# A fused linear-attention and mixture kernel: the written-out order of all engines is replaced by another one

## The chip, the cores and the metric

The kernel runs on one core of a Trainium2 chip. The metric is the device time of one launch in microseconds (us); lower is better. Each of the core's engines works through a queue of its own, and semaphores tie the queues together: TensorE (PE) multiplies matrices, VectorE (DVE), ScalarE (ACT) and GpSimd (POOL) work elementwise, SyncE (SP) issues the transfers.

## The reference

Two stages. A recurrence with a state of 48x48 for each of 4x8 heads runs over 768 steps; its output, 384 wide, goes through four attention experts, of which the two with the largest gate count for a row.

```python
for t in range(S):                                   # S = 768, D = 48
    cur = einsum('bhd,bhe->bhde', u * k[t], v[t])
    y[t] = einsum('bhd,bhde->bhe', r[t], state + cur)
    state = w[t][..., None] * state + einsum('bhd,bhe->bhde', k[t], v[t])
x = y as (B, S, 384)
logits = x @ w_gate                                  # E = 4 experts, the top 2 kept
for e in range(E):                                   # Hd = 64
    q, k, v = x @ wq[e], x @ wk[e], x @ wv[e]
    a = softmax(causal(q @ k.T / 8))
    ye = a @ v @ wo[e]
    out += gate weight of e (if in the top 2) * ye
```

## The kernel before

The work is cut into eight units, a batch and a half of the sequence (384 steps) each. In a unit the recurrence goes over four pairs of heads. The 384 steps of a pair are taken in six chunks of 64: DVE and POOL build products of decays (`w`, `suf`), decayed keys (`kt`) and decayed receptances (`pre`) from the loaded tile `lt`; PE transposes the keys (`ktp`, copied to `kts`), forms what each chunk adds to the state (`ups`), and the products of scores inside a chunk (`aps`, masked into `am`, one `aps` for two pairs of heads); DVE carries the state over the six chunks, one update `wst = wst * suf + ups` each (L366), so that each update reads the one before it of the same pair; PE joins state and scores to the output (`yps`). The bonus term with `u` is a reduction over a head, `rk`, on DVE (L499, one instruction) or on ACT (L497, six), and a scaling of the values with it, `ux` (L506, six instructions on ACT). Then a unit's `xn` is transposed (`xp`, copied to `xh` and `xl`) and goes through the experts: projections of queries and keys (`pp`, L625), values and gate logits (`vp`, L657, copied to `v_sb`), scores (`sp`, L721), maximum on DVE and exponential on ACT (`a`), transposes of `a` (`tp`, copied to `ATa` and `ATb`), the product with the values (`yp`, L778), gates, and the output projection (`op`, L846).

What runs on which engine, and in which order, isn't decided by a scheduler. `Plan.add` numbers some 2,100 operations and notes what each reads and writes. A table, `ORDER`, lists them all as a letter for the engine and a number (`V` DVE, `A` ACT, `P` PE, `G` POOL, `S` SP, `X` left out), and `Plan.order` walks that table; the engines' queues are this list taken apart. Buffers are handed out along the list, the one that has been free longest first:

```python
        for e, n in listed:
            o = ops[n]
            for s in o["slots"]:
                if s.idx is None and e:
                    s.idx = free[s.tag].pop(0)
            o["e"] = o["how"] = e
            if e == "PE":
                o["how"] = last = way(last, o["mode"])
            finish(o)
```

PE's operations have a mode: `F` uses the whole array, `Q`, `S`, `T` and `V` use tilings of it (`Q` 64x64, `S` and `T` 64 rows, `V` 64 columns). A transpose runs in 64-row pieces or, where the operation ahead of it uses the whole array (`way`), in one piece. A load on SP waits for the last PE operation but one that stands ahead of it in the list. Ten multiplications at the start (`warm`) have no reader.

Of the kernel before, what the change touches and what calls it, by code (L numbers as in the profile page):

```python
# [941 lines left out]
S110 S111 V2 V1 V117 V118 V119 V114 S3 V121 V120 V123 P5 S136 S197 S112 V139 V142 V122 V143 V146 V144 V148 V147 V145 V149 S137 S113 P6 S170 V176 V173  # L942
V177 V180 V178 V124 V182 S171 P7 S195 P8 P115 P9 P126 P140 A127 A141 A116 A0 P128 P10 S138 S235 P151 A152 P11 P12 P153 P13 A125 A129 P14 P185 A186
P187 A150 S99 A188 V130 S250 V154 V155 V156 V157 V158 V159 V131 V132 V133 V134 P161 G181 G198 G206 G205 V160 V243 V238 V179 G135 V164 V162 V189 G201
V183 X165 X163 P174 A175 P199 A200 V190 S289 V202 V207 S196 V239 V203 V204 V258 V208 V253 V254 P166 A167 P210 V211 V191 V240 S172 S4 P168 A169 P229
A209 A230 A184 G242 V244 V192 V241 V257 P212 G259 G194 S236 S251 P220 V193 V213 V214 V215 V216 V217 V297 G292 G219 G296 S304 V218 V221 P265 X222 P225
V223 V255 V293 S290 V246 V247 V256 V245 V261 V260 V262 X224 P227 A267 S367 A266 P268 A226 S352 A100 P231 A232 A228 A248 P1131 P1066 P233 P1127 P1067
P1070 P1128 P1071 A263 A234 A249 A102 A264 V269 V275 V270 V276 V271 V272 V294 V277 G298 G307 V273 V312 V300 V278 V308 S305 V311 V313 V295 G274 G299
G374 V279 V309 P281 V284 V282 S104 S252 P1068 P1129 S237 P319 P1072 P1132 P1133 X285 X283 V310 V370 V280 V355 V314 V301 V371 A320 A1069 A1130 A1073
A321 P335 A338 A1134 A105 P322 S368 V315 V356 V316 P1086 P1087 P1088 V329 V323 V317 V324 V330 V331 V325 V302 A1089 A318 G101 G359 S306 G360 G361 P286  # L950
V336 S291 V326 V327 V332 A303 S353 V287 V333 V288 X337 V378 G334 G328 G339 S408 S423 G376 P1074 P1097 P1106 P1115 V1098 V1100 V1109 V1091 V1107 V357
V1118 P343 A1101 A1090 P1075 P1104 A344 A1119 V1116 V345 P1080 P1081 P1076 P1082 A1108 A1099 A1117 P1122 A1084 A1105 A1123 V358 V103 V106 P340 P1111
A1077 A1110 A1083 A1078 A1112 G363 V341 V1085 V342 V372 V1079 V375 V411 V1092 V379 V373 V362 V416 P1120 A1121 P1113 P1102 S369 A1114 A1103 P382 P349
P346 S409 A383 P1124 P1125 P1126 A350 A347 A384 P385 A386 A393 A1165 A380 V351 V348 G377 P1135 P1144 V430 V412 V426 V415 G364 G1093 G419 S473 G431
P1259 P1260 P1261 V1136 V1147 V387 V1138 V394 V413 S107 V388 V395 V1145 V389 A1137 A1148 A381 A1262 A1094 A1139 P400 V401 V403 P1195 P1196 P1197 P1151
V414 V417 S488 V427 P1153 A1152 P1142 A1198 X404 X402 G418 G432 V396 V428 V397 S424 S354 V1156 V390 V398 V1154 V391 V429 V420 V433 P1205 P1191 P1192
P1193 P1206 P1207 A365 A1143 A1146 P1149 S410 V480 V1095 A1194 S542 A1157 A1150 A1209 P1222 P1140 A366 A1141 A1208 A1155 V421 P456 P1211 P1212 P1213
V1225 V1223 V457 G399 G1096 G476 X458 P1231 A459 P1160 S527 A108 A1161 V434 V477 V491 V392 V1232 V1234 V478 G460 G495 P1158 P438 P405 V435 V482 V479
V1167 V1210 V492 A422 A440 A439 A1159 P441 V407 V1216 S489 V406 V442 V449 V450 V443 V451 V444 V493 V452 V436 A1226 A1235 P1162 P1163 P1164 A1215 A1166
A1214 A1224 P1242 G549 G1168 G497 G481 G109 G483 P1169 P1263 P1264 A1233 A437 V445 V1170 V1243 V446 V453 V447 V454 P1171 P1265 S425 P1239 V1172 S474  # L960
V1245 V494 V496 V499 V498 V545 G455 P503 A1266 A1240 A1173 A504 A1241 A505 P1175 P1199 P1200 P1201 P1229 A1230 A1203 P1236 A1237 A1238 V1176 V530
A1177 G448 G1178 G534 G550 G1174 G535 G500 G484 S605 P519 P1227 P1267 A1228 A1202 A1244 A1246 V520 V522 P506 P461 X523 X521 V1204 V1268 V513 V1270
V507 V508 V463 V509 V510 V514 S490 V511 V515 V516 V462 V517 V531 V485 S543 S590 V532 V546 V1217 V533 V536 S592 P1247 P1179 P1180 P1183 P1184 P1250
A1248 A1249 A501 A1185 A1251 A1252 A502 P1276 P467 S528 A468 V1279 V1277 V469 V486 V547 A1280 A1181 P1253 P1254 P1255 G551 G593 G1218 G518 P470 P557
P464 A471 A465 V472 V466 V537 V553 V548 V512 S475 V538 V608 A559 A1219 A558 V554 P1256 P1257 P1258 P1284 A1304 S661 A1269 A1271 A1285 A1286 P1287
# [138 lines left out]
```

## Time and profile before

| | |
|---|---|
| median of 3 runs | 325.13 us (324.5 to 327.95) |
| the profiled execution | 323.68 us |
| its span, first to last instruction | 321.9 us |
| PE busy | 308.9 us |
| DVE busy | 265.3 us |
| ACT busy | 237.2 us |
| POOL busy | 133.6 us |

The median is what counts. The profiled execution is one more run, and durations and waits below are its own. "Busy" is the time in which at least one instruction of an engine ran; PE's instructions overlap in its pipeline, so the distance from one start to the next says what one costs.

### The profile page before, as it was taken

The numbers are of one execution on the slowest core, as the hardware profiler recorded it, in microseconds if no ns is written. First come the engines' busy times: TensorE is split into PE (matmuls) and PEld (weight loads), VectorE is DVE, ScalarE is ACT, GpSimd is POOL, SyncE is SP. The second block draws the span as 40 slices with busy tenths as digits, with TensorE's granted clock in tenths as the row PEclk, the third lists the DMA queues.
The fourth block names the chain that finished last, engine by engine and source line by source line (L and its number), as shares of the span: only waits on it lengthen the run. The fifth ranks groups of instructions, "written<-read, shape, count | busy, mean of one in ns | idle before, by whom it ended". The sixth has DMA issues, their size and how long they took to land.

```text
span 321.9 us, 12978 instructions
## 1 busy us (share of the span) xinstructions
PE 308.9 (96%) x5179; PEld 245.1 (76%) x5179; DVE 265.3 (82%) x872; ACT 237.2 (74%) x835; POOL 133.6 (42%) x267
## 2 busy tenths in 40 slices
PE   4989999998999999999999999998999999999995
PEld 2678677876877987898768767997769686777775
DVE  6998999999999999999988899986774745637743
ACT  1526988899989988887889888455978546775762
POOL 2224454545655446635555755285622010120220
PEclk9987999999999999999999999999999999999999
DMA  7687655674554564665571474340200010001022
GB/s 249 238 289 250 213 184 207 200 245 131 150 171 149 176 222 155 214 219 136 163 256 36 158 275 119 119 131 22 95 2 2 24 52 2 0 4 49 2 100 73
DMA packets 18204, 44.13 MB, mean 137 GB/s; under 512 B 2144, under 2 KB 10080, under 8 KB 18144
## 3 DMA queue, kind: packets, MB, share of 16 engines
q1 hardware_dynamic: 18144, 43.30, 41.6%
q8 instruction: 41, 0.67, 0.9%
q14 instruction: 19, 0.16, 0.2%
HBM read 38.58 MB, written 4.72 MB: 135 GB/s over the span
## 4 chain that ended last, share of the span: by engine, by line
PE 80%; DVE 13%; DMA 2%; issue 2%; ACT 1%; SPq 0%
PE pp L625 14%; PE yp L778 12%; PE sp L721 12%; PE op L846 8%; PE vp L657 7%; PE tp L184 5%; PE tp L180 4%; PE aps L532 4%; PE ups L355 3%; PE yps L310 3%; PE yps L308 3%; DVE wst L366 2%; DMA lt<-in_wkr_dram 2%; DVE am L537 2%; DVE suf L467 2%
## 5 line engine op out<-in xcount | busy, mean ns | idle before, releaser
L736 ACT ACTIVATE a<-a,mx 128x128 f32<-128x128 f32 (+5 forms) x96 | 64.2, 671 | 8.4 <-DVE mx L731 8.1
L731 DVE CUSTOM_DVE_ANT_0 a<-sp,causal 128x128 f32<-128x128 f32 (+5 forms) x96 | 56.9, 618 | 14.8 <-PE sp L721 9.0
L188 ACT COPY ATa<-tp 128x512 f32<-128x512 f32 (+3 forms) x79 | 36.9, 482 | 16.7 <-PE tp L184 11.0
L721 PE MATMUL sp<-K,Q 64*128 64x384 f32 (+4 forms) x256 | 46.3, 471 | 0.0
L366 DVE SCALAR_TENSOR_TENSOR wst<-wst,suf,ups 112x48 f32<-112x48 f32 x160 | 37.2, 257 | 2.1 <-PE ups L355 0.4
L506 ACT ACTIVATE xn<-nat,rk 128x48 f32<-128x48 f32 x156 | 37.8, 330 | 0.4 <-DVE rk L499 0.4
L778 PE MATMUL yp<-ATa,v_sb 128*64 128x384 f32 (+2 forms) x240 | 35.6, 430 | 0.0
L625 PE MATMUL pp<-xh,wh_qk 128*128 128x384 f32 x84 | 31.1, 371 | 0.0
L625 PE MATMUL pp<-xh,wl_qk 128*128 128x384 f32 x84 | 28.3, 337 | 0.0
L625 PE MATMUL pp<-xl,wh_qk 128*128 128x384 f32 x84 | 28.3, 337 | 0.0
L184 PEld LDWEIGHTS tp<-ident,a 64*128 64x128 f32 x456 | 19.6, 138 | 11.0 <-ACT ATa L188 3.2
L721 PEld LDWEIGHTS sp<-K,Q 64*128 64x128 f32 x256 | 20.8, 187 | 8.8 <-issue 2.3
L310 PE MATMUL yps<-ys,pre 64*64 64x48 f32 (+1 forms) x704 | 25.1, 222 | 1.2 <-issue 1.2
L308 PE MATMUL yps<-vy,am 64*64 64x48 f32 x768 | 25.5, 222 | 0.0
L778 PEld LDWEIGHTS yp<-ATa,v_sb 128*64 128x64 f32 x240 | 15.2, 136 | 12.7 <-issue 9.9
L310 PEld LDWEIGHTS yps<-ys,pre 64*64 64x64 f32 (+1 forms) x704 | 22.2, 136 | 3.3 <-issue 2.4
L184 PE MATMUL tp<-ident,a 64*128 64x64 f32 x456 | 23.2, 227 | 1.3 <-ACT ATa L188 1.2
L308 PEld LDWEIGHTS yps<-vy,am 64*64 64x64 f32 x768 | 23.0, 136 | 0.0
L188 ACT COPY kts<-ktp 128x384 f32<-128x384 f32 x29 | 13.5, 487 | 13.0 <-PE ktp L180 9.7
L478 POOL TENSOR_TENSOR kt<-lt,suf 128x384 f32<-128x384 f32 x16 | 15.0, 935 | 14.5 <-DVE suf L467 3.9
L537 DVE TENSOR_TENSOR am<-aps,dec_mask 128x384 f32<-128x384 f32 (+1 forms) x34 | 18.6, 553 | 2.2 <-PE aps L532 1.6
L480 POOL TENSOR_TENSOR pre<-lt,w 128x384 f32<-128x384 f32 x13 | 12.1, 940 | 19.9 <-DVE w L471 9.5
(154 smaller groups left out, 854.3 us busy)
## 6 DMA issues: line engine op xcount, KB each, us to landing
lt<-in_wkr_dram SPq DMA_DIRECT2D x31, 583.0 KB, 4.9
nat<-in_nat_dram SPq DMA_DIRECT2D x28, 432.0 KB, 3.7
vy<-in_vY_dram SPq DMA_DIRECT2D x32, 144.0 KB, 3.2
out_dram<-ob SPq DMA_DIRECT2D x24, 192.0 KB, 2.1
w_qk<-in_wqk_dram SPq DMA_DIRECT2D x1, 768.0 KB, 4.3
nat<-in_nat_dram SPq DMA_DIRECT2D x4, 144.0 KB, 5.3
w_vg<-in_wvg_dram SPq DMA_DIRECT2D x1, 390.0 KB, 4.0
lt<-in_wkr_dram SPq DMA_DIRECT2D x1, 384.0 KB, 3.2
```

The costliest lines, as they stand in the source:

```text
L184: nc.tensor.transpose(o()[:, h * 512 + i * 64:h * 512 + i * 64 + 64], src[r], ident[r, r])
L188: nc.scalar.copy(o, i)
L308: nc.tensor.matmul(to, am()[k, c, :], vy()[k, c, :], start=zero and x == 0, stop=not first and i == 2 and x == len(group) - 1)
L310: nc.tensor.matmul(to, pre()[r, c, 0:C], ys()[r, c, :], start=i == x == 0, stop=False)
L366: nc.vector.scalar_tensor_tensor(new, ws[0:112, c0 + c - 1, :], sfv()[0:112, c, 0:1], upk()[0:112, o], op0=ALU.mult, op1=ALU.add)
L506: nc.scalar.mul(xn()[:, i, (2 * p + h) * D:(2 * p + h + 1) * D], v()[:, i, h, :], rk()[:, i, h:h + 1])
L625: nc.tensor.matmul(pp()[:, 0:384], w[:, qk, k, cs], x()[:, k, :], start=(k == j == 0), stop=(k == j == 2))
L721: nc.tensor.matmul(spv(x)[:, h, :], q()[p, t], flat(k())[p, o], start=True, stop=True)
L731: nc.vector.tensor_tensor_reduce(out=a()[:, 0:n].rearrange("p (a n) -> p a n", a=np_), in0=spv(x), in1=causal[:, S - n:S].rearrange("p (a ...
L736: plan.add("exp", {"ACT": t_exp(n)}, lambda e, x=x, y=y, mx=mx, a=a: nc.scalar.activation(a()[:, 0:n], a()[:, 0:n], AF.Exp, bias=mx(), sca ...
L778: nc.tensor.matmul(yp()[e * 64:e * 64 + 64, lo:hi], v_sb[ep]()[:, j, e * 64:e * 64 + 64], at, start=(j == 0), stop=(j == nj - 1))
L846: nc.tensor.matmul(op()[:, 0:DM], y()[:, t], w[:, ep, :], start=(j + ep == 0), stop=(j == 2 and ep == 1))
```

## The change

`ORDER` is replaced as a whole; nothing else differs. Both tables hold the same operations, and a few stand on another engine: of the 32 reductions and scalings that can choose, ACT has 18 `rk` and 27 `ux` (17 and 30 before), DVE has 14 `rk` (15 before), and the copies out of PE's results that ACT does are 439 operations of ACT in all (434 before). DVE has 729 operations (728), POOL 163 (170), PE 572 in both. Along PE's list the tiling changes 157 times (162 before). The beginning of the table:

```diff
 ORDER = """
-S110 S111 V2 V1 V117 V118 V119 V114 S3 V121 V120 V123 P5 S136 S197 S112 V139 V142 V122 V143 V146 V144 V148 V147 V145 V149 S137 S113 P6 S170 V176 V173
+S110 S111 V2 S3 V117 S136 V118 V114 V119 V121 V122 V123 V120 P5 V142 V139 V143 S170 V146 V147 V176 V124 S4 S137 V144 V148 S112 V173 V145 V177 V180
```

What that makes of the queues is shown at three places. The first is DVE's queue at the first state updates of the first unit; `wst_82` is the state of the first pair of heads, `wst_83` that of the second. Before:

```order
L478 TENSOR_TENSOR kt_166<-lt_154,suf_160 128x2x192
L366 SCALAR_TENSOR_TENSOR wst_82<-wst_82,suf_117,ups_216 112x48
L190 COPY wst_83<-ups_245 112x48
L366 SCALAR_TENSOR_TENSOR wst_83<-wst_83,suf_139,ups_245 112x48 x5
L366 SCALAR_TENSOR_TENSOR wst_82<-wst_82,suf_117,ups_216 112x48 x4
L376 TENSOR_TENSOR ys_341<-wst_83,suf_139 112x240
```

And now (the pair of rows at the end stands there twice more):

```order
L478 TENSOR_TENSOR kt_160<-lt_136,suf_153 128x2x192
L366 SCALAR_TENSOR_TENSOR wst_82<-wst_82,suf_118,ups_198 112x48 x2
L469 RECIPROCAL inv_pre<-suf_153 128x6
L190 COPY wst_83<-ups_228 112x48
L366 SCALAR_TENSOR_TENSOR wst_82<-wst_82,suf_118,ups_198 112x48
L366 SCALAR_TENSOR_TENSOR wst_83<-wst_83,suf_134,ups_228 112x48
```

The two pairs' updates stood in two blocks; now they alternate, until the last of the second pair's.

The second place is ACT's queue in the second unit's recurrence, around the split of the value weights (`wh_vg`). Before:

```order
L543 COPY am_861<-aps_836 64x384 x2
L188 COPY K_864<-pp_699 128x384
L268 CAST wh_vg<-w_vg 128x780
L188 COPY v_sb_908<-vp_894 128x128
L506 ACTIVATE xn_721<-nat_753,rk_900 128x48 x6
L506 ACTIVATE xn_721<-nat_614,rk_906 128x48 x6
```

And now:

```order
L497 ACTIVATE nat_603,rk_818<-nat_603 128x48 x6
L188 COPY kts_825<-ktp_807 128x384
L188 COPY kts_827<-ktp_807 128x384
L188 COPY K_833<-pp_558 128x384
L736 ACTIVATE a_885,asum_894<-a_885,mx_886 128x128
L543 COPY am_900<-aps_835 64x384 x2
L634 ACTIVATE Q_1002<-pp_560 128x384
L497 ACTIVATE nat_760,rk_1004<-nat_760 128x48 x6
L268 CAST wh_vg<-w_vg 128x780
L188 COPY v_sb_1012<-vp_896 128x128
L188 COPY v_sb_1014<-vp_896 128x128
L506 ACTIVATE xn_711<-nat_603,rk_818 128x48 x6
```

The two reductions (L497) were DVE's before, two of its `TENSOR_REDUCE` (L499); now they stand in ACT's queue, ahead of the copies of the values and of the scalings that read them.

The third place is SP's queue at the very start, the loads of the second and third pair of heads and what stands between them. Before:

```order
L197 DMA lt_129<-in_wkr_dram 128x1166
L197 DMA vy_131<-in_vY_dram 128x288
L197 DMA nat_120<-in_nat_dram 128x288
L197 DMA nat_134<-in_nat_dram 128x288
L197 DMA vy_150<-in_vY_dram 128x288
L197 DMA lt_154<-in_wkr_dram 128x1166
```

And now:

```order
L197 DMA lt_116<-in_wkr_dram 128x1166
L197 DMA lt_136<-in_wkr_dram 128x1166
L893 DMA u_sb<-in_uN_dram 128x384
L197 DMA nat_132<-in_nat_dram 128x288
L197 DMA nat_120<-in_nat_dram 128x288
L197 DMA lt_156<-in_wkr_dram 128x1166
```

The third pair's tile (`lt_154` before, `lt_136` now) moved ahead of four smaller loads.

## Rows read from the trace of the kernel before

**Rows 1.** The page: span, busy times, and slices of a fortieth of the span.

```profile
span 321.9 us, 12978 instructions
PE 308.9 (96%) x5179; PEld 245.1 (76%) x5179; DVE 265.3 (82%) x872; ACT 237.2 (74%) x835; POOL 133.6 (42%) x267
...
GB/s 249 238 289 250 213 184 207 200 245 131 150 171 149 176 222 155 214 219 136 163 256 36 158 275 119 119 131 22 95 2 2 24 52 2 0 4 49 2 100 73
```

**Rows 2.** By stage: stretch, length, busy PE, PEld, DVE, ACT, POOL; clock, DMA.

```profile
0.00:20.00 20.00, 13.99 (x224) 9.84 (x226) 16.65 (x51) 7.05 (x26) 5.93 (x19) 1.00 0.77 261
20.00:60.00 40.00, 38.58 (x879) 29.71 (x877) 38.40 (x123) 29.74 (x120) 16.19 (x21) 0.91 0.64 212
60.00:100.00 40.00, 39.08 (x681) 30.61 (x681) 38.41 (x130) 36.13 (x135) 24.02 (x44) 1.00 0.59 180
```

**Rows 3.** Timeline of PE around 85 us: start, length, then what.

```profile
85.17 1.18 PE L532 MATMUL aps<-pre,kt 64*64 64x64 f32 x48
```

**Rows 4.** Timeline of DVE around 85 us.

```profile
84.83 0.55 DVE L480 TENSOR_TENSOR pre<-lt,w 128x384 f32<-128x384 f32 x1
85.30 0.35 DVE L465 TENSOR_TENSOR w<-lt 128x199 f32<-128x199 f32 x1
85.57 0.55 DVE L832 TENSOR_TENSOR yr<-gb,yr 128x384 f32<-128x384 f32 x1
```

**Rows 5.** Waits of PE from 85 to 322 us: total, times, longest.

```profile
PE yps L310 <- issue: 1.2, 1, 1.2
```

**Rows 6.** Busy time in three more stretches, columns as in rows 2.

```profile
21.70:28.40 6.70, 5.92 (x128) 5.08 (x126) 6.37 (x22) 3.71 (x15) 2.20 (x4) 0.50 0.72 245
56.40:94.80 38.40, 37.48 (x692) 30.17 (x690) 37.21 (x127) 33.72 (x132) 21.69 (x37) 1.00 0.61 187
85.20:318.00 232.80, 231.48 (x3695) 185.64 (x3695) 186.08 (x616) 176.75 (x600) 95.84 (x198) 1.00 0.34 108
```

**Rows 7.** Timeline of DVE at two places with state updates.

```profile
14.30 2.54 DVE L366 SCALAR_TENSOR_TENSOR wst<-wst,suf,ups 112x48 f32<-112x48 f32 x9
16.75 0.79 DVE L376 TENSOR_TENSOR ys<-wst,suf 112x240 f32<-112x240 f32 x1
...
33.42 1.25 DVE L366 SCALAR_TENSOR_TENSOR wst<-wst,suf,ups 112x48 f32<-112x48 f32 x6
34.59 0.19 DVE L469 RECIPROCAL inv_pre<-suf 128x6 f32<-128x6 f32 x1
```

**Rows 8.** Timeline of DVE at a bonus reduction.

```profile
44.36 0.45 DVE L499 TENSOR_REDUCE rk<-nat 128x6 f32<-128x288 f32 x1
44.73 0.90 DVE L366 SCALAR_TENSOR_TENSOR wst<-wst,suf,ups 112x48 f32<-112x48 f32 x4
```

**Rows 9.** Timeline of ACT: two reductions' first piece, the copy behind them, two scalings.

```profile
33.15 0.26 ACT L497 ACTIVATE nat<-nat 128x48 f32<-128x48 f32 x1
...
35.87 0.46 ACT L188 COPY xh<-xp 128x384 f32<-128x384 f32 x1
...
45.66 2.81 ACT L506 ACTIVATE xn<-nat,rk 128x48 f32<-128x48 f32 x12
```

**Rows 10.** Timeline of PE around 217 us.

```profile
217.06 0.28 PE L657 MATMUL vp<-wl_vg,xh 128*128 128x260 f32 x1
217.17 0.28 PE L657 MATMUL vp<-wh_vg,xl 128*128 128x260 f32 x1
217.39 0.84 PE L355 MATMUL ups<-nat,kts 64*64 64x48 f32 x39
```

**Rows 11.** DVE's first operation for the second pair; loads: count, size, landing.

```profile
7.70 0.56 DVE L448 TENSOR_TENSOR nat<-lt 128x384 f32<-128x384 f32 x1 [0.42 <-DMA lt<-in_wkr_dram]
...
lt<-in_wkr_dram SPq DMA_DIRECT2D x4, 583.0 KB, 5.9
```

**Rows 12.** Waits of DVE up to 86 us: total, times, longest.

```profile
DVE am L537 <- PE aps L532: 0.9, 2, 0.7
...
DVE a L731 <- PE tp L180: 0.3, 1, 0.3
```

More of the change, by code (lines that the diff above doesn't have):

```diff
@@ L946 @@
[L946 to L953, printed above, removed]
@@ new lines @@
+V279 V282 G299 G313 V310 V374 V314 V355 S104 V284 G280 S237 G359 P1072 P1068 P1128 S252 P1129 P319 A1069 A1073 A317 A320 A321 P1133 P1097 A1134 X283
+X285 P335 P322 V274 V356 V1100 V300 V370 S368 V301 A1101 P1086 P1087 P1088 A338 S291 V371 V329 V323 V357 V1098 V330 V324 V331 V325 S473 V336 V326
+V1091 P286 V327 V332 V333 V288 V287 S306 P1106 P1115 X337 V1107 V1109 V1118 P343 A1130 A302 A105 A1090 A1089 A318 A303 P1080 P1104 S408 P1081 P1074
+P1082 P1075 P1076 G101 G360 G339 G375 G328 V361 V103 V1116 V1105 A1110 A1108 P1111 S353 A344 A1119 A1117 A1083 A1112 G334 V106 V358 A1078 P340 G362
@@ new lines @@
+P470 A465 A471 A558 A559 P1255 P1256 P1257 P1258 G1218 V486 V547 V466 V472 P1284 A1271 A1219 A1304 A487 A1285 A1286 V548 V597 V537 V552 P1287 V594
+V538 V1220 V595 V1288 V1290 S661 P1187 P1188 P1330 S646 A1289 P560 P573 G512 G599 G553 G539 P524 V561 V567 V562 S544 S529 V568 V563 V569 V554 V608
+V596 V664 V669 V526 V525 V570 V564 V571 V565 V576 V574 V555 G1221 G598 G572 G612 G566 S662 X577 X575 A1189 A540 A541 V609 V600 V610 V649 V611 V650
+V668 P1331 P1391 P1332 P1392 A1333 A1291 P581 P1272 S591 P1393 P1395 P1396 A582 A1273 A1278 V613 V1306 A1394 P1295 P1292 P1334 P1397 A1297 A1296 P578
@@ new lines @@
+V827 P1519 P1520 P1521 P1522 A1555 A1553 S901 G880 V967 V911 V875 V908 P1538 P1545 P1559 A1561 A1546 A1560 A1547 A1568 P1719 S845 P1720 P1721 A1722
+A842 V1570 V905 V1539 G1571 P1625 S1450 V1628 V1626 V912 P1556 P914 S965 P1548 P1572 P1723 P1724 P1725 A1558 A916 V953 V895 V1025 V1573 V954 P1574
+A915 A1557 P917 G909 G956 P932 V913 A1550 A1549 V968 V971 A918 V1575 V933 V919 S950 G896 V955 V1021 S1003 P881 V958 V935 V882 A1576 A1726 A897 A898
+A1627 A1629 G975 G973 P1562 P1563 P1564 P1565 P1566 P1567 V883 V969 V970 P979 P1634 P1578 V925 V981 V1635 A1569 S966 V1579 A980 A1580 S1446 P1727
@@ L1019 @@
+P2095 P2092 P2093 P2094 V2112 A2113 P2096 P2097 P2125 S1978 P2098 S1974 P2099 P2100 V2126 V2114 P2131 P2127 P2119 P2115 P2116 P2120 A2132 V2133 A2134
+V2128 A2129 V2135 A2117 S2118 A2121 V2130 S2122 P2136 P2137 A2138 S2139
 """
```

130 lines of the change are left out of this document (62 added, 68 removed).

## The prediction

> **What bounds the kernel now.** I read the page's head first, then the table by stage, then single places. The head says that TensorE (PE) is busy for 308.9 of 321.9 us and VectorE (DVE) for 265.3 [rows 1]. The table says where each matters [rows 2]: from 20 to 100 us both are full (PE 38.58 and 39.08 of each 40 us, DVE 38.40 and 38.41) and ScalarE (ACT) rises from 29.74 to 36.13, while from 85.2 to 318 us PE is busy for 231.48 of 232.80 and DVE for 186.08, 80% [rows 6]. So the first third has two full engines, the rest has one.
>
> Which of the two leads in the first third is read at one place. The seventh product of scores (`aps`, L532) starts on PE at 85.17 [rows 3]. The last of its inputs, a `pre` on DVE, runs from 84.83 for 0.55 us [rows 4]. PE began with the other pair's `pre` 0.2 us before this one ended, so it took the work up as DVE let go of it: up to here DVE's queue sets the time. Behind it PE waits once, for 1.2 us [rows 5]. The time is then DVE's queue up to that `pre`, with its waits, plus PE's work behind that `aps`, plus the tail. I call this `pre` and its `aps` the hinge. The order keeps both; the `pre` stands in row 242 of DVE's queue before and after.
>
> **DVE up to the hinge: -1.6 us.** A state update (`wst`, L366) that reads the one directly ahead of it costs more than one that doesn't. Nine updates take 14.30 to 16.75, seven of them ahead of an update that reads them; six take 33.42 to 34.59, one of them so [rows 7]. Two equations, 7x + 2y = 2.45 and x + 5y = 1.17, give x = 0.30 and y = 0.17 us. I counted the neighbours in DVE's queue of which the second reads the first: 25 up to the hinge before, 15 now (55 and 36 in all). Most are such updates; the first place in the section on the change shows how two chains are now laid alternately. Ten times 0.12 us is -1.2.
>
> The kinds of operations shift too. Four bonus reductions (`rk`, L499) stood ahead of the hinge, now one does; one takes 44.36 to 44.73 [rows 8], so three are -1.1. One key copy leaves for ACT: -0.47, by the `pre` of the same 384 columns, 84.83 to 85.30 [rows 4]. In come, net, three decay products of 192 or 199 columns at 0.27 (85.30 to 85.57 [rows 4]): +0.8, and two copies of 128 columns, at most 0.27 each: I take +0.4. That is -0.4, and -1.6 with the neighbours.
>
> **ACT: 0 in the sum.** The three reductions go to ACT, where they are dearer: twelve pieces, two reductions, take 33.15 to 35.87, 1.36 us each [rows 9]. With one more scaling of the bonus (`ux`, two take 2.81 us [rows 9]) and the copies, ACT has 5.7 us more to do by what is PE's 94.8 us of before. What hides it is ACT's idle time: 2.6 us lie ahead of 56.4 us, and 20 to 60 us leaves 10.3 idle [rows 2]; 3.1 us lie between 56.4 and 94.8, where ACT is busy for 33.72 of 38.40 [rows 6], so 4.7 are free. Queued behind a reduction are `v_sb` copies and two `ux` (second place), for which the value products and the next `xp` wait. If that cover is gone it costs what the second rival gives.
>
> **PE: -0.3 us.** Changes of tiling fall from 162 to 157, but behind the hinge they are 120 before and 121 now. One costs 0.1: inside one tiling value products follow each other after 0.11 us (217.06, 217.17), ahead of another tiling after 0.22 (217.17, 217.39) [rows 10]. That alone is +0.1. Pricing every PE operation behind the hinge at its spacing in the trace of before with the same neighbours, some 229 us in both, gives -0.3 to -1.0, by how pairs that occur once are priced. I take -0.3, the end nearest to the count of changes.
>
> **SyncE's loads: 0.** The third pair's load now stands right behind the second's (third place). DVE's wait for the second, to 7.70, stays, since that load keeps its place [rows 11]. The third is 583 KB [rows 11]; at 289 GB/s, the best slice of the start [rows 1], it lands 2.0 us later, at 9.7, and DVE asks for it about 9.4. The other end is no wait, at a rate over this mean. I take 0 and keep +0.3 for the range.
>
> **DVE's waits: unchanged.** Up to 86 us there are four rows of waits for PE, from 0.9 us for `am` to 0.3 for `a`, together 2.0 [rows 12]. A new order makes its own; the ends are none (-2.0) and twice as many (+2.0).
>
> **Sum.** The profiled execution took 323.7 us, its span of 321.9 [rows 1] and 1.8 around it. Less 1.6 and 0.3 it is 321.8. The median of the three runs, 325.13, stands 1.45 above that execution; the same 1.9 off it give 323.2, which is the time I predict. About 1% (3.2 us) is what a measurement of this kernel can tell from no change.
>
> **The rivals.** *ACT becomes the bound.* This ends on the other side. In the stretch 56.4 to 94.8 ACT would need 33.72 + 3.1 = 36.8 us. The fullest it ran is 36.13 of 40, 90% [rows 2]; at that share 36.8 take 40.8 us in place of 38.4. PE then reaches the stretch's end 2.4 us later than before in place of 1.9 earlier: 327.5. It decides once ACT is busy for more than about 90% of the stretch. Should none of the 5.7 be hidden, less about 1.1 by which PE's own work up to there shrinks, it is 4.6 later: 329.7. For it: the 3.1 are two thirds of what is free. Against: PE and DVE still wait for little there, and the early 2.6 fall where ACT is idle.
>
> *DVE's waits for PE vanish*, since PE is ahead with its first projections: 2.0 us more are saved, 321.2. For it: the longest, 0.7 us, is for an `aps` [rows 12] that runs while the granted clock is 0.50 [rows 6]. Against: waits elsewhere can take their place.
>
> *PE's clock falls in a dense stretch.* From 21.7 to 28.4 us the granted clock is 0.50, the lower level of 1.2 GHz, after a start in which PE was busy for 13.99 of 20 us [rows 2, 6]. DVE led there, so little was lost. The new order begins its projections just behind that stretch; if the drop comes so much later that it covers them, half of 6.8 us is lost: 3.4, less the 1.9, or 326.6 at the worst, with nothing lent by DVE. For it: other first operations on PE. Against: DVE's queue gains only 1.6 us, so the start keeps its shape.
>
> *PE isn't the bound behind the hinge.* Then DVE's whole queue sets the time. There 19 fewer dependent neighbours give -2.3, while four more `uk`, one more `ur`, three more decay products of each of two kinds, fewer `rk`, `kts` and `ev` and the rest add 1.8: -0.5, or 324.6. Against it PE's 231.48 of 232.80 [rows 6]. The Trainium skill (Trainium Kernel Development and Optimization, Performance Expectations) calls matmul busy time a bad metric, because matmuls are pipelined, and the busy share of weight loads a good one. By that rule PE, whose loads are busy for 185.64 of these 232.80 us, would have a fifth to spare, and this rival would hold. The spacings disagree: matmuls of one tiling start every 0.11 us without a gap.
>
> **How the numbers follow.** The forecast has a chance of 0.41, ACT 0.25, vanished waits 0.16, the clock 0.13, DVE's whole queue 0.05. The forecast's own range is 321.2 to 325.2, by the ends of the waits, the 0.3 of the load and the -1.0 of PE. The range over the cases is 320.2 to 328.0: it leaves out ACT with nothing hidden and vanished waits together with PE's -1.0. Faster by over 1%, below 321.9: the vanished waits and a little of the forecast, 0.21. Slower by over 1%, above 328.4: the worse part of ACT and of the clock, 0.09. Within 1%: 0.70.
>
> **What would show it.** Right: the hinge `aps` starts some 1.6 us earlier, near 83.6, with its `pre` on DVE ending at that moment; state updates of the start at 0.17 apart; PE behind it within 0.5 us of before and again with one wait. ACT busy for more than 35 of 38.4 us up to the hinge, and PE or DVE waiting for `ATa`, `kts` or `v_sb` copies there, would show the second rival. A granted clock of 0.5 behind 29 us would show the clock's rival. The forecast is wrong if the hinge comes no earlier, or if what it gains is lost again before 180 us, while DVE is still full.

## The result, and the profile after

Measured beside each other, 20 times each, the kernel before has a median of 325.19 us (323.8 to 330.0) and the changed one 325.25 (320.2 to 328.0). The ratio of the two is given as 0.988 (0.984 to 0.991), measured a second time 0.987 (0.981 to 0.992). It flatters the change: the times of the changed kernel fall into two groups, 320.2 to 322.3 (12 of 26) and 324.8 to 328.0 (14), and the ratio sets the lower group alone against nearly all executions of before, whose times run on from 323.4 to 330 without a gap. By all times that were taken in this study, 26 of the changed kernel and 112 of the one before, the means are 324.05 and 326.23, 0.7% less (0.5% and 1.2% in the two series taken side by side); the lower group has its median at 321.8, the times of before under 326.5 (a border drawn here, where there is no gap) have theirs at 324.9, 1.0% less. Ratios below are to the kernel before, measured beside each run; the changed kernel itself was measured in the first two series only.

The first profiled execution of the changed kernel took 325.28 us, one of the upper group. Its page, with the lines that answer to [rows 1] and the clock by slices:

```profile
span 323.2 us, 12948 instructions
PE 309.7 (96%) x5172; PEld 245.2 (76%) x5172; DVE 267.8 (83%) x874; ACT 234.8 (73%) x835; POOL 130.1 (40%) x260
...
PEclk9999999699999999999999999999999999999999
```

One slice of the clock stands out, the eighth (56.6 to 64.6 us). Waits of PE in this stretch (total, times, longest), then PE's timeline there, then DVE's:

```profile
PE yps L308 <- issue: 2.9, 1, 2.9
```

```profile
53.44 0.30 PE L310 MATMUL yps<-ys,pre 64*64 64x48 f32 x8
53.56 0.29 PE L308 MATMUL yps<-vy,am 64*64 64x48 f32 x7
56.72 0.24 PE L308 MATMUL yps<-vy,am 64*64 64x48 f32 x1 [2.87 <-issue]
```

```profile
53.69 0.14 DVE L663 COPY lg<-vp 128x4 f32<-128x4 f32 x1
56.99 0.82 DVE L328 TENSOR_TENSOR xn<-yps,xn 128x288 f32<-128x288 f32 x2 [3.15 <-PE yps L308]
```

Between the seventh and the eighth of eight equal small products PE stands still for 3 us and waits for nothing that another engine owes it; DVE stands with it. From 55.5 us on, while PE still stands, the granted clock is the lower of its two levels (stretch, length, busy PE, PEld, DVE, ACT, POOL; clock, DMA):

```profile
21.40:55.50 34.10, 30.52 (x753) 23.27 (x753) 31.72 (x101) 27.63 (x125) 12.82 (x15) 1.00 0.70 225
55.50:62.30 6.80, 5.41 (x54) 3.73 (x54) 4.87 (x15) 4.23 (x19) 0.79 (x1) 0.50 0.32 107
```

The hinge of the prediction starts at 89.56 us here, against 85.17 [rows 3]. That is no property of the new order, as the next profiled execution of the same kernel shows (322.34 us, span 320.5): it has no such standstill, the clock stays at 1.00, and the hinge starts at 85.92. Its rows for the hinge, of PE and of DVE, answer to [rows 3, 4]:

```profile
85.66 0.33 PE L824 MATMUL gb<-gT,sel 128*128 128x128 bf16 x3
85.92 0.93 PE L532 MATMUL aps<-pre,kt 64*64 64x64 f32 x48
```

```profile
84.84 0.55 DVE L480 TENSOR_TENSOR pre<-lt,w 128x384 f32<-128x384 f32 x1
```

From here on this second execution (e1 below) is compared with the one of before (323.68 us), neither with a standstill near 54 us. The span is 1.4 us shorter: 320.5 against 321.9 [rows 1].

**Where it went.** Up to the end of the hinge's `pre` (85.38 before, 85.39 now), busy times in the columns above; before, then now:

```profile
0.00:85.38 85.38, 77.11 (x1486) 59.47 (x1486) 79.44 (x258) 60.15 (x237) 37.80 (x69) 0.96 0.65 215
```

```profile
0.00:85.39 85.39, 76.42 (x1460) 59.45 (x1461) 77.82 (x259) 63.48 (x268) 34.00 (x63) 1.00 0.67 215
```

DVE has 1.62 us less to do and stands idle for 7.57 in place of 5.94, 1.63 more. All of its saving went into waits. Nor does DVE set the hinge any more. Before, the `aps` started 0.2 us ahead of the end of its `pre`; now it starts 0.53 us behind it, and PE, which had gaps of 0.84 us in the stretch from 70 us on, has none (before, then now):

```profile
70.00:85.38 15.38, 14.54 (x256) 11.73 (x248) 14.64 (x50) 13.97 (x44) 9.37 (x17) 1.00 0.49 145
```

```profile
70.00:85.39 15.39, 15.39 (x273) 12.27 (x270) 14.85 (x50) 15.32 (x57) 8.05 (x16) 1.00 0.37 117
```

In all twelve profiled executions of the new order, edited or not, the hinge's `aps` starts 0.50 to 0.55 us behind the end of its `pre`: PE, not DVE, is the later one there.

Behind the hinge's start the span has 234.6 us in place of 236.7: that is the gain, 2.1. From the hinge to PE's last product, before, then now:

```profile
85.17:318.50 233.33, 231.97 (x3696) 185.81 (x3695) 186.11 (x616) 176.78 (x601) 95.84 (x198) 1.00 0.34 108
```

```profile
85.92:317.17 231.25, 230.55 (x3709) 183.98 (x3707) 189.50 (x615) 170.36 (x566) 96.42 (x197) 1.00 0.34 109
```

PE is busy for 1.42 us less and idle for 0.70 us in place of 1.36. Nearly all of its idle time is one standstill in each: before, the wait in [rows 5] (1.43 us from the last start to the next), now a shorter one at another place (0.87 us):

```profile
218.81 0.29 PE L310 MATMUL yps<-ys,pre 64*64 64x48 f32 x3
220.32 0.32 PE L310 MATMUL yps<-ys,pre 48*64 48x48 f32 x3 [1.22 <-issue]
```

```profile
116.14 0.27 PE L184 MATMUL tp<-ident,a 64*128 64x64 f32 x2 [0.65 <-issue]
```

The fall in PE's work is steady. Its steps from start to start behind the hinge, less the standstills, add up to 231.5 and 231.4 us in the two profiles of before and to 230.0 and 229.9 in the two of the changed kernel.

**What the standstills have in common** shows when PE's instructions are counted from the start (the matmul and weight-load rows and the few event rows of its queue). The instructions themselves come by a DMA queue, the page's "q8 instruction": 41 packets of 16 KB, 256 instructions each (PE's 10,509 rows before make 41 blocks of 256). The list below, worked out from the trace rows, gives for some executions where PE stands, for how long from one start to the next, after which instruction, and when the packet that carries the next ones moves:

```
kernel                 PE stands from, for    instruction  of 256   packet moves
before                 218.88   1.43 us       8385         193      217.77 to 218.89
before, again          55.27    1.67          1984         192      54.57 to 55.51
                       222.96   1.16          8384         192      221.82 to 222.74
changed, first         53.63    3.09          1985         193      54.30 to 55.26
changed, second (e1)   -                      (1985)                51.83 to 52.71
                       115.27   0.87          4289         193      113.55 to 114.67
```

Each standstill lies at instruction 192 or 193 of a block of 256 (the counts differ by one, since a trace can lack a record), and PE goes on 1.4 to 1.5 us after the packet has landed. In the second execution the same packet began 2.5 us earlier, and PE passed the place at 54.93, 2.2 us after it had landed. The border at 8,385 is weak in the order of before alone: its packet begins 3.7 and 3.9 us behind the border ahead of it in the two profiles of before, 0.6 to 0.9 us in all twelve of the new order, which all pass. The one at 4,289 is weak in the new order alone: nine of its eleven profiles (e3 aside) stand there, for 0.5 to 1.2 us, neither of the two of before. The Trainium skill (Runtime: NRT & Kernel Launch, Instruction fetch mechanics) says that instructions are refilled in 16 KiB blocks of 256 while the current one runs, and that crossing a border is mostly hidden. The block size agrees with the packets here. Most borders are crossed without a standstill here too; those in the list cost 0.9 to 3.1 us each.

### The profile page after: what moved, and what is told of

The parts are those of the page before. It is cut to its first block, busy times and chain, and to the rows that moved or that the text cites. A ratio compares the mean times of both kernels' runs of the same rounds, so it can differ in the third digit from the quotient of the medians.

```text
span 323.2 us, 12948 instructions
## 1 busy us (share of the span) xinstructions
PE 309.7 (96%) x5172; PEld 245.2 (76%) x5172; DVE 267.8 (83%) x874; ACT 234.8 (73%) x835; POOL 130.1 (40%) x260
## 4 chain that ended last, share of the span: by engine, by line
PE 86%; DVE 6%; ACT 3%; DMA 2%; issue 2%; POOL 1%; POOLq 0%; ACTq 0%
PE pp L625 15%; PE sp L721 13%; PE yp L778 13%; PE op L846 8%; PE vp L657 8%; PE tp L184 5%; PE aps L532 4%; PE ups L355 4%; PE tp L180 3%; PE yps L308 3%; PE yps L310 3%; DMA lt<-in_wkr_dram 2%; PE rk L456 1%; PE ktp L180 1%; PE ktp L184 1%
## 5 line engine op out<-in xcount | busy, mean ns | idle before, releaser
L736 ACT ACTIVATE a<-a,mx 128x512 f32<-128x512 f32 (+5 forms) x96 | 64.0, 669 | 12.5 <-DVE mx L731 12.5
L731 DVE CUSTOM_DVE_ANT_0 a<-sp,causal 128x256 f32<-128x256 f32 (+5 forms) x96 | 57.1, 617 | 13.8 <-PE sp L721 11.0
L778 PE MATMUL yp<-ATa,v_sb 128*64 128x384 f32 (+2 forms) x240 | 37.0, 442 | 0.0
L366 DVE SCALAR_TENSOR_TENSOR wst<-wst,suf,ups 112x48 f32<-112x48 f32 x160 | 35.6, 257 | 1.6 <-ACT wst L188 0.4
L506 ACT ACTIVATE xn<-nat,rk 128x48 f32<-128x48 f32 x138 | 33.5, 331 | 1.2 <-DVE rk L499 1.1
L184 PEld LDWEIGHTS tp<-ident,a 64*128 64x128 f32 x472 | 20.0, 141 | 11.7 <-issue 5.8
L721 PEld LDWEIGHTS sp<-K,Q 64*128 64x128 f32 x256 | 21.1, 187 | 10.2 <-issue 3.2
L310 PE MATMUL yps<-ys,pre 64*64 64x48 f32 (+1 forms) x704 | 24.0, 220 | 0.8 <-DVE ys L376 0.8
L310 PEld LDWEIGHTS yps<-ys,pre 64*64 64x64 f32 (+1 forms) x704 | 21.5, 134 | 3.1 <-issue 1.4
L184 PE MATMUL tp<-ident,a 64*128 64x64 f32 x472 | 23.3, 230 | 0.2 <-DVE inv_pre L469 0.2
L537 DVE TENSOR_TENSOR am<-aps,dec_mask 128x384 f32<-128x384 f32 (+1 forms) x36 | 19.8, 552 | 2.5 <-PE aps L532 2.1
L480 POOL TENSOR_TENSOR pre<-lt,w 128x384 f32<-128x384 f32 x15 | 14.3, 955 | 15.4 <-DVE lt L476 8.0
L835 POOL TENSOR_TENSOR yl<-yr,yh 128x384 fp32r<-128x384 f32 x8 | 8.0, 1015 | 30.9 <-ACT yh L834 29.9
```

Source lines behind the costliest of these rows:

```text
L184: nc.tensor.transpose(o()[:, h * 512 + i * 64:h * 512 + i * 64 + 64], src[r], ident[r, r])
L310: nc.tensor.matmul(to, pre()[r, c, 0:C], ys()[r, c, :], start=i == x == 0, stop=False)
L366: nc.vector.scalar_tensor_tensor(new, ws[0:112, c0 + c - 1, :], sfv()[0:112, c, 0:1], upk()[0:112, o], op0=ALU.mult, op1=ALU.add)
L506: nc.scalar.mul(xn()[:, i, (2 * p + h) * D:(2 * p + h + 1) * D], v()[:, i, h, :], rk()[:, i, h:h + 1])
L721: nc.tensor.matmul(spv(x)[:, h, :], q()[p, t], flat(k())[p, o], start=True, stop=True)
L731: nc.vector.tensor_tensor_reduce(out=a()[:, 0:n].rearrange("p (a n) -> p a n", a=np_), in0=spv(x), in1=causal[:, S - n:S].rearrange("p (a ...
```

## Experiments

No run leaves out a part of the computation; what some add or drop are the multiplications without a reader at the start (`warm`). Theory: the upper times come from a block that arrives too late where PE runs through 256 short instructions quickly, and the order's own gain at the hinge is eaten by waits for PE. Rivals: the big loads delay the block; the clock; ACT.

**e1, the changed kernel again**, no edit.

> The changed kernel as it is, once more. In its profiled execution PE stood still for 3.09 us at 53.6 us, in the middle of one product (yps), at a place where it waits for no other engine. The theory of the code blocks: PE's instructions come in pieces of 16 KB, 256 instructions each; the piece due there began to move at 54.30, 7.1 us after the previous one was begun, because loads filled the transfer engines (other pieces: 0.1 to 3 us). It says: an execution without a stretch of low clock (span near 319.8) has this piece's transfer begin before 51 and no standstill at 53.6; an execution near 325 has it. The rival, that the clock falls by itself and the standstill is a part of that: a fast execution still has the standstill of about 3 us at the same place, and differs in the clock alone.

Median 322.14 (320.3 to 325.7, 6 runs). The profile is the one used above: with the block early there is no standstill at this place and no low clock. The packet began at 51.83, somewhat later than expected. Same program, same place: what differs is when the packet moves.

**e2, a load moved.** `S473`, a 583 KB tile issued at 46 us, goes behind PE's output products (`P340`):

```diff
-V325 S473 V336
+V325 V336
-P340 G362 S423
+P340 G362 S473 S423
```

> One load alone (a tile lt of 583 KB, issued at 46.0 us and read first at 62.1) is moved behind the product yps that starts at 52.2 us. The code-block theory: the transfer engines are idle from 47 to 50 us, so the block asked for at 47.2 begins to move before 49, PE doesn't stand still at 53.6, and all rounds lie near the faster group of the changed kernel's times (321.6 to 322.3), none near 325 to 328 for this reason. The rival, that the clock falls by itself: times in two groups as before, about half of them at 325 and over. A third way: the load moved is late for its reader; then DVE waits for lt at 59 to 62 us, up to 2 us, and the time is 1 to 2 us over the faster group.

Median 322.9 (320.9 to 326.8, 7 runs), ratio 0.987 (0.981 to 0.993). Three of the seven are above 326, and the profiled one stands still for 2.28 us at 54.56, instruction 1985; its packet began at 54.43. So this load is not the cause: a miss for the theory that the load delays the block.

**e3, the borders moved.** Each `warm` is followed by four products of one column, 80 instructions more in front of everything, so that other work lies on the borders:

```diff
-lambda e, w=w: nc.tensor.matmul(w()[:, 0:512], wz[:, 0:128], wz, start=True, stop=True)
+lambda e, w=w: [nc.tensor.matmul(w()[:, 0:n], wz[:, 0:128], wz[:, 0:n], start=True, stop=True) for n in (512, 1, 1, 1, 1)]
```

> Each of the ten multiplications at the start that nobody reads is followed by four of one column: 80 more instructions for PE in a time in which it waits (2.7 to 6.4 us), nothing else. The code-block theory: the borders of the blocks of 256 instructions fall 80 instructions earlier in the work. In the trace of the changed kernel the 256 instructions between two such borders would then take only 1.8 to 1.9 us at four places (107.6, 131.2, 142.5 and 199.6 us), where a block needs about 0.6 to start, 0.95 to land and 1.45 until PE goes on, 3.0 in all: PE stands still for 1.1 us or more at each of the four, in the middle of small products, and for some tenths at 212 and 156.8; together 5 to 8 us, so 326 to 330 us. The rival, that code has no part in it: no standstill, the time as that of the changed kernel, 321.6 to 322.3 in its faster group.

330.5 (328.5 to 332.6, 4 runs), ratio 1.013 (1.007 to 1.019). PE's waits over the whole span (total, times, longest), and one place in its timeline:

```profile
PE yps L308 <- issue: 4.2, 2, 2.9
...
PE ups L355 <- issue: 1.8, 1, 1.8
...
PE yps L310 <- issue: 1.4, 1, 1.4
PE vp L657 <- issue: 1.4, 1, 1.4
```

```profile
107.66 0.32 PE L310 MATMUL yps<-ys,pre 48*64 48x48 f32 x7
110.93 0.47 PE L308 MATMUL yps<-vy,am 64*64 64x48 f32 x8 [2.94 <-issue]
```

Standstills at 32.5 (1.99 us), 107.8 (3.16), 135.9 (1.62), 148.9 (1.43) and 207.5 (1.48), all at instruction 193 of a block. Four of the five places had been worked out from the first trace of the changed kernel. The place at 54 has none. This is the experiment that settles the mechanism: nothing of the order was touched, 40 small products without a reader (80 instructions) moved the borders, and the span is 330.7 us against 320.5 in e1, 10.2 more. Its five standstills add up to 9.7 us, e1 has one of 0.87.

**e4, the kernel before again**, no edit.

> The kernel before, once more. Its profiled execution took 323.7 us, the fastest of all it has shown; most take 324.5 to 328.8. The code-block theory: an execution of 326 us and more shows PE standing still in the middle of small products at further borders of its blocks of 256 instructions, beside the 1.4 us at 218.9, or a second stretch of low clock behind such a standstill; together 2 to 4 us over the execution shown. The rival: the start alone is later, the first loads landing 1 to 2 us later, with no standstill but the one at 218.9.

324.97 (323.8 to 328.5, 8 runs), ratio 0.999 (0.995 to 1.004). Its profiled execution has a span of 325.7:

```profile
PE yps L310 <- issue: 2.4, 2, 1.5
```

Two standstills, at 55.27 (1.67 us) and 222.96 (1.16), and the clock at 0.51 from 57.6 to 61.1. So the border near 55 us is weak in the kernel before too, where its first profile had passed it; the one at 8,384 is in both of its profiles.

**e5, the two chains in blocks again.** The alternation shown at the first place of the change is undone, nothing else:

```diff
-V178 V154 V132 V155 V133 V156 V134 V157 V158 V159 V179
+V178 V132 V133 V134 V154 V155 V156 V157 V158 V159 V179
```

> The changed kernel with the first unit's two chains of state updates in two blocks again, as before the change: five more updates read the one directly ahead. By the prediction's step (0.13 us for each, with DVE leading) the seventh aps comes 0.65 us later, counted from DVE's first state update, and the time rises by that. The rival: in the changed kernel DVE stands still 0.6, 0.4 and 1.2 us around these updates, waiting for ups, for an ACT copy and for the first aps; then the alternation bought nothing, the first am starts at the same distance from the first state update (8.3 us) in both, and the time is the same within 0.3.

325.1 (321.6 to 327.4, 10 runs), ratio 0.995 (0.990 to 1.000). The profiled execution (321.56) has no standstill at 54. Up to the end of the hinge's `pre`, as above:

```profile
0.00:84.78 84.78, 75.89 (x1459) 59.19 (x1461) 78.17 (x259) 63.49 (x268) 34.02 (x63) 1.00 0.67 216
```

DVE has 0.35 us more to do than in e1 (78.17 against 77.82) and yet the hinge comes at the same distance from the first state update: 71.53 us against 71.58 (before: 71.29). The busy time that alternating saves buys nothing there, where PE is the later one.

**e6, three reductions (`rk`) back on DVE:**

```diff
-A317
+V317
-A302
+V302
-A421
+V421
```

> The changed kernel with three bonus reductions (rk) ahead of the seventh aps back on DVE, at their places in the order. By the prediction's step DVE leads there, so the seventh aps comes 1.1 to 1.35 us later, and so does the end. The rival that ACT is the bound in this stretch: ACT has 4.1 us less to do, so the aps comes no later or earlier, and the time falls or stays.

328.1 (323.5 to 330.4, 10 runs), ratio 1.004 (0.999 to 1.009). Measured from the first state update, an `aps` in the middle (70.39 us in e1) comes 1.0 us later with two of them ahead, and the hinge, with all three, 2.5 later. With the third there is a new wait on PE ahead of the hinge:

```profile
PE gb L824 <- ACT K L188: 1.4, 1, 1.4
```

```profile
83.33 1.32 PE L180 MATMUL tp<-ident,a 128*128 128x128 f32 x9
86.01 0.33 PE L824 MATMUL gb<-gT,sel 128*128 128x128 bf16 x3 [1.36 <-ACT K L188]
```

The wait starts on DVE: ACT's scalings wait 3.2 us for the `rk`, and the copy `K` stands behind them in ACT's queue:

```profile
82.76 2.84 ACT L506 ACTIVATE xn<-nat,rk 128x48 f32<-128x48 f32 x12 [3.20 <-DVE rk L499]
85.50 0.46 ACT L188 COPY K<-pp 128x384 f32<-128x384 f32 x1
```

So the reductions given back to DVE cost more than their own 0.45 us apiece (1.35), since others wait for them. The rival that ACT becomes the bound falls: with less to do on ACT the hinge comes later.

**e7, a longer start for PE.** The first four `warm` products become fp32 with 320 columns:

```diff
+wide = causal[:, 0:640].bitcast(F32)
+nc.tensor.matmul(w()[:, 0:320], wide[:, 0:128], wide, start=True, stop=True) if i < 4 else
 nc.tensor.matmul(w()[:, 0:512], wz[:, 0:128], wz, start=True, stop=True)
```

> The first four of PE's multiplications without a reader are made longer (320 columns in fp32 in place of 512 in bf16, the same number of instructions), so that PE works from 1.4 to about 5.7 us in place of 1.4 to 3.3; nothing else. In the trace of the changed kernel PE's first aps takes 2.84 us at 17.9 (1.63 at 16.0 before), since full clock comes at 21.4 us (14.8 before), and DVE waits 1.2 us for it. The theory that this late rise cost the start its gain: with more activity the clock rises before 18 us, the first aps takes 1.0 to 1.7 us, DVE's wait for am falls below 0.4, and the time is about 1 us under the faster group of the changed kernel (321.8), near 320.8. The rival: the clock's rise is not brought forward by this, or DVE then waits elsewhere; the time is the same within 0.3.

323.2 (320.6 to 326.8, 11 runs), ratio 0.990 (0.985 to 0.995), no better than the changed kernel. The clock, columns as above:

```profile
5.90:12.70 6.80, 3.13 (x57) 1.98 (x56) 5.52 (x16) 1.26 (x4) 0.00 (x0) 1.00 0.99 304
12.70:26.40 13.70, 13.28 (x292) 12.39 (x289) 12.26 (x42) 5.31 (x23) 4.59 (x7) 0.50 0.67 219
```

It rose earlier, at 5.9, while PE still waited for its first tiles, and was back at the lower level when the work came. A miss.

**e8, another start.** The first 190 entries of the table are re-sequenced so that DVE's early waits for PE go (its first line):

```diff
-S110 S111 V2 S3 V117 S136 V118 V114 V119 V121 V122 V123 V120 P5 V142 V139 V143 S170
+S110 S111 A0 P8 V2 V1 S3 P9 S136 V114 S170 P115 V117 V121 V118 A116 S4 P5 V122 S137
```

> The changed kernel with the first 190 entries of the order put in another sequence (same operations, same engines, loads in the same sequence): PE's bonus products (rk) stand ahead of the first transposes again, in a time in which PE waits, the first aps ahead of the third pair's ups, so that DVE waits less for ups, for the copy by ACT and for the first aps. The theory that waits of the start ate what DVE's shorter queue gained: DVE's waits for PE and ACT up to 30 us fall from 2.6 to under 1.2 us, the seventh aps comes 1 to 2 us earlier than the 85.3 to 85.9 us of the changed kernel's undisturbed executions, and the faster group of times lies near 320 in place of 321.6. The rival, that PE is full from 29 us on and leads as much as DVE: the waits go, the seventh aps comes no earlier, the time stays within 0.5 of 321.6. Times over 324.5 should stay as frequent as before, since the standstill at 53.6 us isn't touched.

323.8 (320.1 to 326.7, 6 runs), ratio 0.989 (0.984 to 0.995). Of DVE's waits for PE up to 50 us one is left:

```profile
DVE wst L190 <- PE ups L355: 0.3, 1, 0.3
```

but PE has one more, for ACT, and the products at `P340` start at 52.64 us against 53.54 in e1 and 52.89 in e5: hardly anything is left of the gain. The time of the hinge can't be compared, since this execution stood still for 2.82 us at 54.03 (instruction 1984); but there too PE has no gap in the 15 us ahead of it, as the rival has it.

```profile
PE sp L721 <- ACT kts L188: 1.3, 1, 1.3
```

**e9, three loads moved**, so that the transfer engines are idle when the block is due:

```diff
-V325 S473 V336
+V325 S408 V336
-P1104 S408 P1081
+P1104 P1081
-P1111 S353 A344
+P1111 A344
-P340 G362
+P340 G362 S353 S473
```

> The changed kernel with three loads moved and nothing else: the lt that was issued at 49.6 us goes to the place of the one issued at 46.0, and that one and the nat issued at 51.9 go behind the product yps at 52.2 us. So no load starts to move between about 50 and 53.5 us. In the executions so far the block of PE's code that is due at 53.6 began to move 0.6 us behind PE's 1,780th instruction (near 51 us), unless a load that started in the same moment came first; then it began 3 us later, behind that load and the next. The code-block theory in this form: the block begins to move before 52.5 in the profiled execution, PE doesn't stand still at 53.6, and of the times none lies at 325 and over (half of them do in the changed kernel as it is). The rival, that loads have no part in the late block: the standstill and the slower group of times stay as frequent. Should the loads moved back be late for their readers at 59 to 61 us, DVE or PE waits there and the time is 1 to 2 us over 321.6.

324.0 (321.6 to 326.0, 12 runs), ratio 0.992 (0.988 to 0.996); half of the times are 324.6 or more. Two stretches of the profile, columns as above (the last two are the share of the DMA engines and GB/s):

```profile
46.00:50.75 4.75, 4.75 (x119) 3.71 (x119) 4.68 (x24) 4.75 (x25) 4.68 (x6) 1.00 0.85 279
50.75:54.20 3.45, 3.39 (x65) 2.61 (x67) 3.45 (x7) 3.45 (x15) 0.43 (x1) 1.00 0.01 2
```

```profile
54.74 0.29 PE L308 MATMUL yps<-vy,am 64*64 64x48 f32 x7
56.82 0.20 PE L308 MATMUL yps<-vy,am 64*64 64x48 f32 x1 [1.79 <-issue]
```

The transfer engines stood idle for 3.45 us and the packet still began only at 54.20; PE stood for 2.01 us at instruction 1984. In these 3.45 us traffic doesn't hold the packet; whether it is asked for late or something else holds it, the trace doesn't tell. The rival holds: nothing shows that the loads have a part.

**e10, e8 and e9 together.**

> Both edits: the new sequence of the first 190 entries and the three loads moved. If both theories hold, all times lie near 320, with none at 324 and over, 5 to 6 us under the median of the kernel before. If only the loads count: 321.6 and one group. If only the start counts: two groups, near 320 and 324.

324.8 (322.0 to 328.9, 12 runs), ratio 0.995 (0.991 to 0.999), with a standstill of 1.98 us at 54.57, packet from 53.94. Not better than either.

**e11, the border moved back by 8.** `P10` to `P13` are left out, two other `warm` products made long to keep the start:

```diff
-P10 P11 P12 P13 A127
+X10 X11 X12 X13 A127
```

> The changed kernel with four of PE's ten multiplications without a reader left out (the sixth to the ninth) and the fourth and fifth made longer (320 columns in fp32 for 512 in bf16), so that PE works about as long in the same places with 8 instructions less. The borders of the blocks of 256 instructions fall 8 instructions later in the work: the border that cut the last product of a yps at 53.6 us, and with it held DVE's xn for 3 us, falls into transposes behind that yps. The code-block theory: the block may still be late, and PE stand still for 1 to 3 us there in some executions, but at its 1,985th plus 8 instructions, and DVE's wait for that yps stays under 0.5 us; the slower group of times moves from 325 to 328 down to 323.5 to 326. The rival, that the place of the border doesn't matter: the two groups stay at 321.6 and 325 to 328, and the standstill is found inside the yps again.

326.2 (322.1 to 327.5, 12 runs), ratio 0.997 (0.992 to 1.001). PE now passes all of the `yps` and stands in the next transposes:

```profile
54.50 0.30 PE L308 MATMUL yps<-vy,am 64*64 64x48 f32 x8
54.73 0.27 PE L184 MATMUL tp<-ident,a 64*128 64x64 f32 x1
57.69 0.64 PE L184 MATMUL tp<-ident,a 64*128 64x64 f32 x13 [2.69 <-issue]
```

The place moved by exactly the eight instructions, so the border is where it was thought to be. The slower times (325.6 to 327.5) did not fall as hoped: DVE gets its `yps` but waits 2.8 us for ACT's `xh` behind it.

**e12, e8's start with four `warm` products fewer.**

```diff
-P10 V143
+X10 V143
-P7 P11 A127 P12
+X7 X11 A127 X12
```

> The new sequence of the first 190 entries, with four of the ten multiplications without a reader left out, so that the borders fall 8 instructions later in the work, as in the run beside it. If both count: a faster group near 320 and a slower one near 323, a median of 321 to 323, 3 to 5 us under the kernel before. If the border's place doesn't count: 320 and 323 to 327, as measured with the new sequence alone.

323.8 (320.2 to 326.8, 6 runs), ratio 0.988 (0.982 to 0.995). The profiled execution stood still for 1.63 us at 53.99 and kept its clock; its span is 320.6. Without the standstill it is 70.7 us from the first state update to the hinge, against 71.6 in e1, so the new start may be worth 0.8 us, an estimate from these two traces. No run beats the changed kernel by more than the measurement can tell.

## Why the prediction was right or wrong

The time, 323.2 predicted, is 0.6% below the first series' median (325.25), 0.3% above the second's (322.14) and 0.3% below the mean of all 26; all of these lie in the range and within 1% of it. Whether the kernel changed by over 1% depends on the measure: by the means it is 0.7%, the case given 0.70, by the ratio 1.2%, the case given 0.21. The way there was right in part only.

**The first third has two full engines, DVE leads.** This is the step that failed. In the trace of before DVE led at the hinge, by 0.2 us; the prediction took it that DVE goes on leading there and that every microsecond of its work ahead of that place counts. In the new order PE is the later one by 0.53 us, without a gap behind 70 us, so less work on DVE didn't bring the hinge forward, and e5's 0.35 us more didn't put it off. Nor does it count where DVE waits for loads or for PE, in the first 25 us above all. DVE's work counts where others wait for it, as in e6.

**DVE's work up to the hinge, -1.6.** Exact in the sum: 79.44 to 77.82. In the disturbed execution it is 77.87. The terms are not as priced: the state updates, 60 in both, are busy for 13.40 us in place of 13.89, 0.5 less, where the neighbours, most of them such updates, were to give 1.2; three `rk` fewer give 1.1, as priced. Undoing the alternation of the first two chains alone (e5) cost 0.35.

**DVE's waits, unchanged.** Wrong by +1.6, if within its end of +2.0. DVE's waits of e1 up to 86 us (total, times, longest), against those of before in [rows 12]:

```profile
DVE w L465 <- DMA lt<-in_wkr_dram: 1.3, 1, 1.3
DVE am L537 <- PE aps L532: 1.2, 1, 1.2
DVE wst L190 <- PE ups L355: 1.0, 2, 0.6
...
DVE nat L448 <- DMA lt<-in_wkr_dram: 0.5, 1, 0.5
DVE wst L366 <- ACT wst L188: 0.4, 1, 0.4
```

Loads cost 1.8 us where they cost 0.4, PE and ACT 2.6 where they cost 2.0; smaller waits that the view doesn't list fell by some 0.4. That is the 1.6, and 1.4 of it is loads, which come and go between executions (below). The longest for PE is for the first `am`. PE at the first `aps`, before and then in e1:

```profile
15.64 0.56 PE L355 MATMUL ups<-nat,kts 64*64 64x48 f32 x24 [0.57 <-ACT kts L188]
16.02 1.63 PE L532 MATMUL aps<-pre,kt 64*64 64x64 f32 x48
```

```profile
17.82 1.33 PE L456 MATMUL rk<-u_t,nat 64*64 64x1 f32 x21
...
19.03 0.94 PE L355 MATMUL ups<-nat,kts 64*48 64x48 f32 x22
19.78 2.84 PE L532 MATMUL aps<-pre,kt 64*64 64x64 f32 x48
```

The new order puts the bonus products (`rk`, L456) ahead of this `aps`, so it starts at 19.78 in place of 16.02. It is also longer: 48 products take 2.84 us, not 1.63 (at the hinge 0.93, at a clock of 1.00). The clock is recorded from 14.8 us on before and from 23.0 in e1, each time with a step up to 1.00, so the `aps` of e1 ran ahead of that step. From the first state update to the third output (`yps`) of the first unit it is 16.9 us in e1 against 15.5 before: 1.5 lost in the first 31 us, and 1.2 won back up to the hinge. e5 and e8 are two sides of it: DVE work added at the start changes nothing, and its waits for PE taken away change little, as PE is full behind them.

**ACT, 0.** Right. ACT is busy for 63.48 us up to the hinge, 3.3 more than before. In the 38.40 us ahead of it ACT is busy for 36.86, 96%:

```profile
47.52:85.92 38.40, 37.78 (x694) 30.52 (x684) 37.65 (x128) 36.86 (x153) 20.78 (x36) 1.00 0.59 188
```

That is over the 35 named as a sign of the rival and over the 90% that was to be its limit, so that limit is none. But none of the waits for `v_sb`, `kts` or `ATa` that were to show the rival reaches 0.5 us on PE or DVE (e1); giving the reductions back made it slower (e6).

**PE behind the hinge, -0.3 (to -1.0).** The work was mis-sized: it falls by 1.4 to 1.5. Of this 0.25 is the hinge's own `aps`, 0.93 us in place of 1.18, which no longer waits half-way for its second input. By start-to-start steps the 162 products `vp` at L657 take 21.07 us in place of 21.93, and the transposes (L180, L184) 0.8 less without the standstill; no run tells which neighbours in the new list do it. The standstills were the term that was left out. [rows 5] showed one, and the prediction counted it as "waits once, for 1.2 us", one wait among others that would be there "again". One wait there is again, but it is another one, 0.6 us shorter. No engine owes it. The one at 8,385 went with the order of before, the one at 4,289 came with the new order, the one near 54 us comes and goes between executions, and all of them move with the number of instructions ahead (e3). PE is busy for 230.55 of 231.25 us there, so the rival by which DVE's whole queue sets the time falls.

**SyncE's loads, 0.** The third pair's load, which the term was about, is waited for in none of these executions. The second pair's, which was to stay, moved: DVE waits for it 1.28 us in e1 and lets go at 8.71, against 0.42 and 7.70 [rows 11]; 1.27 in e5, 0.68 in e2, nothing in the first execution. So the price is 0 to about 1 us by execution, where 0 to 0.3 had been kept. Whether the load behind it takes its bandwidth wasn't tried.

**The sum.** -1.9 predicted; -1.4 in e1's span, -2.2 in e5's. Right in size and wrong in place: none of it at the hinge, which the prediction had named as what would prove it wrong, and all of it behind. That the sum fits is luck: a gain that didn't come (-1.6) was replaced by work of PE (-1.1 beyond the -0.3) and a shorter standstill. The stated range of the forecast, 321.2 to 325.2, also leaves out two of the ends it names: with PE's -1.0 it begins at 320.5, with the load's +0.3 it ends at 325.5.

**The clock's rival** named the right symptom, a clock of 0.5 behind 29 us, in the first execution, and the wrong cause: PE fell to the lower level not in a dense stretch, but 1.9 us into a standstill of 3 us. From the first state update to the hinge the first execution needs 77.1 us, e1 71.6: 3.1 us for the standstill and about 2.4 of the 3.4 that half the clock over 6.8 us can cost.

**What stays open.** The 3.1 us between the medians of the lower times are covered by the two traces only in part: this pair, 322.34 and 323.68, lies at the top of the one group and near the bottom of the other. What the other executions of before lose has one trace, e4's. Which executions stand still near 54 us is not settled either. Of the profiled ones of the new order (e3 aside) those with a span of 323.1 or more all do, those of 321.7 or less do not, but for e12. The packet begins to move when PE is at its 1,760th to 1,792nd instruction in e1, e5, e6 and in the profile of before, which all pass, and at its 1,886th to 1,985th in all others but e3, where other work lies there; never while PE is between these. Traffic doesn't decide it (e2, e9); what does was not found.

## What to carry to other kernels

An "issue" wait inside a run of equal small matmuls is a term of its own: count PE's instructions to it, and if it falls at the same place of a block of 256, look through the trace, block by block, at when the packet begins and lands against when PE reaches the border: where it stood in these traces, PE went on 1.1 to 1.6 us after the landing. Any edit that shifts the count of instructions moves these places. A saving in an engine's busy time is a gain only at places where that engine is late, and only until another one is later: a lead of 0.2 us does not carry a saving of 1.6. Read for each such place what the engine waits for, from the first microsecond on, before adding savings up at one place far behind. And take a second profile of an unchanged kernel before explaining the first.

## What the runs showed of the hardware

PE stands still at some block borders, for 1.2 to 3.2 us in most of the cases, and for 0.5 to 1.2 us at instruction 4,289 of the new order (0.87 in e1). The price of a block in e1, by its earlier packets: 0.7 us from the border before it to the packet's start (border at 44.94, start at 45.65), some 0.95 for the packet (51.83 to 52.71 is 0.88), and 1.1 to 1.6 from its landing to PE's next instruction in the executions that stood still: together about 3 us, an estimate from these rows. In e3 PE ran through 256 instructions in less than that. The other standstills come from a packet that began late, 2.1 to 7.2 us behind its border; why it did stays open. A late packet is no harm by itself: at 3.35 us (e1) and 4.3 us (before) behind its border PE still passed, at 7.1 it stood for 3.1.

A standstill can cost twice. During the 3.09 us of the first execution and the 3.16 us of e3 the granted clock went to the lower level, from 55.5 to 62.3 and from 110.6 to 114.0 us; it also fell 0.7 us behind the 1.67 us of e4. Behind the 1.43 us of before and the 1.63 of e12 it stayed at 1.00. The standstill comes first: PE stood from 53.63 us on, the clock fell at 55.51. This fits the two groups of times of the changed kernel, which nothing lies between.
